# Cosine attention followed by a mixture of depths, one core: PV output of a head pair in one PSUM bank, a bank of its own for the last score block, two buffers of scaled q and k, fetched rows transposed, a new slot order

## The chip, the core and the metric

The kernel runs on one core of one Trainium2 chip. The metric is the device time of one execution in microseconds, lower is better; the number for a kernel is the median of its runs. Beside it stands one profiled execution with its trace. A span is the time from the first to the last instruction in the trace.

## What is computed

```python
def _attn_ref(q, k, v, tau):                     # 8 batches, 12 heads, 448 tokens, 64 wide
    q_n = q / (norm(q, axis=-1) + 1e-06);  k_n = k / (norm(k, axis=-1) + 1e-06)
    attn = softmax(q_n @ k_n.T / tau)            # tau = 0.1
    return attn @ v
def _moe_ref(x, w_gate, w1, w2, capacity):       # x: (8, 448, 768), F = 1024, capacity 128
    for b in range(B):
        top_idx = 128 rows of x[b] with the highest score x[b] @ w_gate
        xe = x[b, top_idx];  ye = relu(xe @ w1) @ w2
        out[b, top_idx] = xe + sigmoid(score) * ye      # other rows: out = x
```

The attention output of a batch, heads side by side, is x of the second part. All inputs and the output are fp32.

## The kernel before

**Tiling.** Two heads of a batch make a pair; there are 48 pairs, 6 per batch. The 448 tokens lie as 3 blocks of 128 and one of 64 (NC = 3, NS = 4, T = 64). Two heads share the 128 partitions of one tile: in the raw tiles head u has its tokens on partitions 64u to 64u+63, seven tokens per partition (NB7). The last 64 tokens of both heads make one shared block, so scores have four blocks: c = 0, 1, 2 hold 128 keys for each head (two matmuls, 64 rows each, side by side in the array, L275), and c = 3 holds 64 keys of both heads in one matmul (L280).

**A slot** is one pass of the loop `for i in range(N + 1)` (near the end of the function). Slot i computes the scores and exponentials of pair i, the PV product of pair i-1, the transposes of pair i+1, the scaling of pair i+2, and the squares for norms of pair i+5. The loop body writes out by hand the order in which instructions enter each engine's queue; every engine works through its own queue in that order.
- *ScalarE*: exponential of block 0 (L288), Square of a later pair's q and k (L187), in every other slot Ln and Exp for norms (L210, L211), exponential of block 3 (L291), of block 1, of block 2 (L288).
- *TensorE*: scores 0; `pv_tails` (L304: 8 matmuls, one for each query block and head, on 64 rows); sums of squares by an identity (L194); `pv` (L315: 24 matmuls of 65 columns; the 65th, a column of ones, gives the softmax sum); any mixture-of-depths work under key "A"; scores 3, 1; the 28 transposes of pair i+1 (L257); scores 2; work under key "B".
- *VectorE*: sums (L202), reciprocals (L220), `pv_evac` (L331, L333), the copy of the transposes to SBUF (L263), and the gate, rank, pick and evacuation steps of the mixture of depths (L361, L416, L424, L455, L457, L459).
- *POOL*: adds 1e-6 to norms (L217), scales q and k into the single buffer `kn` (L230), casts v (L237), casts x to bf16 (`half_x`, L354), splits gates (L371 to L374), issues the indirect DMAs (L515, L711, L726).
- *SP*: loads q, k and v (L98, L108) for a ring of 4 groups of 3 pairs, and stores x (`store_x`, L346 and L347).

**PSUM** has 8 banks: 2 score buffers of two banks (`sc`), 2 banks for the PV output (`o_ps`, one per head), one for transposes (`qkT_ps`), one for the mixture of depths (`m_ps`). The sums of squares and scores 3 live in the slot's second `sc` buffer. A second copy of the last 64 queries makes query block 3 also 128 wide: `qc(3)` is `slice(S - P, S)`, so its output lies on all partitions.

**The mixture of depths of batch b** starts when its six pairs are done, at slot s = 6(b+1), and is spread over later slots by `at(slot, key, function)`; `run(i, key)` emits what is due. The dicts `late`, `mid`, `early` and `last` give the offsets to s: four `gate` products in slots 2 to 5, `rank_rep` (scores spread to all partitions) in 5 B, `rank_count` and `pick` (a 0/1 matrix `sel`) in slot 6, `select` (row numbers and gate values of the 128 rows) in 7 A, `gather` (rows of `xh` picked and transposed in one go by matmuls with `sel`, 24 in all, L473) in 7 B and 8 A, `ffn1` twice (24 matmuls, L491), `ffn2` twice (8 matmuls of 384 columns, L500), then `scatter` (L515), which adds the rows onto `out` in DRAM. x itself has been stored to `out` by `store_x` in slot s. The last batch comes after the loop: it also stores x to `x_copy`, fetches its rows from there (L711), adds them in SBUF and writes them plainly (L726).

Of the kernel before, what the change touches and what calls it, by code (L numbers as in the profile page):

```python
# [14 lines left out]


@with_exitstack
def kernel(
# [48 lines left out]
    ps_m = ctx.enter_context(tc.tile_pool(name="ps_m", bufs=1, space=PSUM))  # L67
    sc_pool = ctx.enter_context(ExitStack())
# [13 lines left out]
    NORMS = [(0, 1), (1, 2), (3, 1), (4, 1)]  # L82
    while sum(NORMS[-1]) < N:
        NORMS.append((sum(NORMS[-1]), min(2, N - sum(NORMS[-1]))))
# [49 lines left out]
    o_ps = ps_o.tile([P, 2, 512], FP32, name="o_ps")  # L134
# [6 lines left out]
    kn = const.tile([P, 2, NB7, Dh], BF16, name="qkn")  # L141
    vo_bufs = [const.tile([P, NB7, E], BF16, name=f"vo{n}") for n in range(NB)]
    for vo in vo_bufs:
        nc.vector.memset(vo[:, :, Dh:E], 1.0)
# [8 lines left out]
    tokc = const.tile([P, NS, 2], BF16)  # L153
    for half in range(2):
        for col, base, step, mult in ((0, 0, 0, 4), (1, NC * half, 1, 3)):
            nc.gpsimd.iota(tokc[half * T:half * T + T, :, col], pattern=[[step, NS]],
                           base=base, channel_multiplier=mult,
                           allow_small_or_imprecise_dtypes=True)
# [23 lines left out]
    ss_tiles, rs_tiles, sq_tiles = {}, {}, {}  # L182

    def square(p):
        gi, g = place[p]
        sq_tiles[p] = prep.tile([P, 2, NB7 * Dh], BF16, name="sq", bufs=3)
        nc.scalar.activation(  # L187
            sq_tiles[p], raw[gi % NRAW][0][:, :, g].rearrange("p a b d -> p a (b d)"),
            AF.Square)
# [8 lines left out]
    def sum_dve(p, dst):  # L198
        n, m = nplace[p]
        if m == 0:  # L200
            ss_tiles[n] = prep.tile([P, 2, 2, NB7], FP32, name="ss")
        nc.vector.tensor_reduce(  # L202
            ss_tiles[n][:, m].rearrange("p a b -> p (a b)"),
            dst.rearrange("p (n d) -> p n d", d=D8), axis=AX.X, op=ALU.add)

    def norm_a(n):
        gn = NORMS[n][1]
        rs = prep.tile([P, 2, 2, NB7], FP32, name="rs", bufs=3)
# [10 lines left out]
    def norm_c(n):  # L219
        nc.vector.reciprocal(norm_of(n), norm_of(n))  # L220

    def scale(p, split=False):
        gi, g = place[p]
        qk = raw[gi % NRAW][0]
        n, m = nplace[p]
        rs = rs_tiles[n]
        parts = (((nc.gpsimd, 0, NC), (nc.vector, NC, NB7)) if split
                 else ((nc.gpsimd, 0, NB7),))
        for eng, b0, b1 in parts:
            eng.tensor_mul(  # L230
                kn[:, :, b0:b1], qk[:, :, g, b0:b1],
# [3 lines left out]
    def values(p):  # L235
        gi, g = place[p]
        nc.gpsimd.tensor_copy(vo_bufs[p % NB][:, :, :Dh], raw[gi % NRAW][1][:, g])  # L237
# [13 lines left out]
    def transposes(p):  # L251
        for a in range(2):
            for s in range(NB7):
                for u in range(2):
                    r = slice(u * T, u * T + T)
                    o = column(a, u, s)
                    nc.tensor.transpose(out=qkT_ps[r, o:o + T], in_=kn[r, a, s],  # L257
# [9 lines left out]
    def scores(i, c, sc=None):  # L267
        qkT = qkT_tiles[i]
        if sc is None:
# [24 lines left out]

    def qc(j):
        return slice(j * P, j * P + P) if j < NC else slice(S - P, S)

    def pv_tails(i):
        ex = exp_tiles[i]
        vo = vo_bufs[i % NB]  # L300
        for j in range(NS):
            for u in range(2):
                r = slice(u * T, u * T + T)
                nc.tensor.matmul(out=o_ps[:, u, j * E:(j + 1) * E],  # L304
                                 lhsT=ex[r, TAIL, qc(j)], rhs=vo[r, NC],
                                 start=(j == 0), stop=False, tile_position=(u * T, 0),
                                 skip_group_check=True)

    def pv(i):
        ex = exp_tiles[i]  # L310
        vo = vo_bufs[i % NB]
        for u in range(2):
            for j in range(NS):
                for c in range(NC):
                    nc.tensor.matmul(out=o_ps[:, u, j * E:(j + 1) * E],  # L315
                                     lhsT=ex[:, 2 * c + u, qc(j)],
                                     rhs=vo[:, u * NS + c], start=False,
                                     stop=(c == NC - 1), skip_group_check=True)
# [3 lines left out]
    x_last = const.tile([P, NS, P], FP32)  # L322
    xh_last = const.tile([P, NS, P], BF16)

    def pv_evac(i):
        b, hp = divmod(i, HP)
        if hp == 0:
            x_tiles[b] = xp.tile([P, NS, D], FP32, name="x_b")
        o = o_ps[:, :, :NS * E].rearrange("p u (j e) -> p j u e", e=E)
        rden = head.tile([P, NS, 2, 1], FP32, name="rden")  # L330
        nc.vector.reciprocal(rden, o[:, :, :, Dh:E])  # L331
        dst = x_last if i == N - 1 else x_tiles[b][:, :, 2 * hp * Dh:2 * (hp + 1) * Dh]
        nc.vector.tensor_mul(  # L333
            dst.rearrange("p j (u d) -> p j u d", u=2),
            o[:, :, :, :Dh], rden.to_broadcast([P, NS, 2, Dh]))

    xh_tiles, st = {}, {b: {} for b in range(B)}
# [11 lines left out]
    def half_x(i):  # L349
        b, hp = divmod(i, HP)  # L350
        if hp == 0:
            xh_tiles[b] = xp.tile([P, NS, D], BF16, name="xh", bufs=3)
# [14 lines left out]
    def rank_prep(b, eng=nc.gpsimd):  # L367
        g = gates[b % 2]
        sg = moe.tile([P, NS, 3], BF16, name="sg")
# [58 lines left out]
    def select(b):  # L428
        sel, sg = st[b]["sel"], st[b]["sg"]
        pk = bank()  # L430
        for o, w, src in ((0, 2, tokc), (2, 3, sg)):
            for j in range(NS):
                nc.tensor.matmul(out=pk[:, o:o + w], lhsT=sel[:, j], rhs=src[:, j],
                                 start=(j == 0), stop=(j == NS - 1))
        gr = moe.tile([P, 1], FP32, name="gr")
        nc.vector.tensor_reduce(gr, pk[:, 2:5], axis=AX.X, op=ALU.add)  # L436
# [3 lines left out]
        nc.vector.tensor_scalar_add(idx, pks, float(b * S))  # L440
# [323 lines left out]
```

## Time and profile before

| | us |
|---|---|
| median of 3 runs | 269.3 (267.12, 269.3, 269.72) |
| profiled execution | 268.42 |
| its span | 266.6 |
| mean granted TensorE clock in it | 0.985 of full speed |
| DMA traffic | 53.18 MB, mean 199 GB/s |
| exponentials of blocks 0 to 2 (L288), 144 of 128x896 | 917 ns each, 125.3 in sum |
| PV matmuls (L315), 1152 of 128x65 | 44.6 in sum |
| tails (L304), 384 of 64x65 | 13.9 in sum |
| scaling (L230), 48 | 1673 ns each, 80.3 in sum |
| evacuation (L333), 47 of 128x512 | 691 ns each, 32.5 in sum |
| casts of x (L354), 47 of 128x512 | 633 ns each, 29.7 in sum |

In the profile, PE stands for matmuls on TensorE, PEld for its weight loads, DVE for VectorE, ACT for ScalarE, POOL for GpSimd, SP for the queue that issues plain DMAs. A line of a timeline reads: start in us, length in us, engine, line of the program, operation, output <- inputs, shape, count, and in square brackets the idle time before it and what ended that. For a matmul "64*128" are the active rows and columns of the array and "64x448" the operand that streams through. Matmuls overlap in the pipeline, so the distance between starts is what one costs. In a list of waits the three numbers are total us, times and longest us.

### The profile page before, as it was taken

The page shows a single profiled execution, that of the slowest core. Times are in us where ns is not written, and L with a number is a line of the kernel's source. Part 1 is how long each engine was busy: PE and PEld are TensorE (multiplying, and loading weights), DVE is VectorE, ACT ScalarE, POOL GpSimd, SP SyncE. Part 2 cuts the span into 40 slices and gives each one's busy share as a digit, 9 for nine tenths or more (in the row PEclk, how much of TensorE's full clock was granted, in tenths as well). Part 3 has the DMA queues.
Part 4 walks back from the last instruction along what each step waited for, and adds up shares of the span by engine and source line. Part 5 has one row for each costly group of instructions (what it writes and reads, how often), then busy time and mean ns, then how long its engine had stood idle before and what let it go on. Part 6 is the DMA issues. An engine that isn't in the chain of part 4 may idle for free.

```text
span 266.6 us, 10588 instructions
## 1 busy us (share of the span) xinstructions
PE 225.2 (84%) x4584; PEld 169.9 (64%) x4584; DVE 175.2 (66%) x472; ACT 203.3 (76%) x322; POOL 168.3 (63%) x234
## 2 busy tenths in 40 slices
PE   7678877586899979999899979998999899989920
PEld 6456655465678557767677757866786667757810
DVE  2424445474977778858877778678876976898401
ACT  3698999897897798888888789779878986683400
POOL 5367676979766568575966667757846885743131
PEclk9999999999999999999999999999999999999995
DMA  7999999999999974799679985999580049047861
GB/s 248 285 286 279 264 254 275 368 260 259 267 285 350 235 161 64 167 276 285 130 153 262 260 203 84 216 283 274 101 192 20 2 61 210 4 61 161 255 116 63
DMA packets 32431, 53.18 MB, mean 199 GB/s; under 512 B 2176, under 2 KB 28672, under 8 KB 31488
## 3 DMA queue, kind: packets, MB, share of 16 engines
q1 hardware_dynamic: 28976, 45.13, 63.9%
q0 software_dynamic: 2992, 6.69, 14.6%
q8 instruction: 36, 0.59, 1.0%
q10 hardware_dynamic: 416, 0.69, 0.7%
q14 instruction: 11, 0.09, 0.1%
HBM read 40.11 MB, written 15.53 MB: 209 GB/s over the span
## 4 chain that ended last, share of the span: by engine, by line
PE 35%; DMA 21%; DVE 16%; ACT 12%; issue 7%; SPq 4%; POOL 3%; POOLq 1%; ACTq 0%
DMA v_raw<-in_v_dram 11%; PE m_ps L491 7%; ACT expS L288 7%; PE m_ps L500 6%; PE sc L275 6%; PE o_ps L315 5%; DVE junk L416 4%; DVE junk L361 3%; DMA qk_raw<-in_k_dram 3%; DMA qk_raw<-in_q_dram 3%; PE sc L194 3%; ACT expS L291 3%; PE qkT_ps L257 3%; DVE xeT L457 2%; DVE x_b L333 2%
## 5 line engine op out<-in xcount | busy, mean ns | idle before, releaser
L288 ACT ACTIVATE expS<-sc 128x896 bf16<-128x896 f32 x144 | 125.3, 917 | 17.0 <-PE sc L275 16.4
L230 POOL TENSOR_TENSOR qkn<-qk_raw,rs 128x896 bf16<-128x896 f32 (+1 forms) x48 | 80.3, 1673 | 36.4 <-PE qkT_ps L257 26.3
L275 PE MATMUL sc<-qkT 64*128 64x448 bf16 x288 | 52.3, 358 | 14.8 <-DVE qkT L263 7.3
L187 ACT ACTIVATE sq<-qk_raw 128x896 bf16<-128x896 f32 x48 | 45.2, 947 | 2.1 <-DMA qk_raw<-in_k_dram 2.0
L315 PE MATMUL o_ps<-vo,expS 128*128 128x65 bf16 x1152 | 44.6, 193 | 1.5 <-issue 1.5
L315 PEld LDWEIGHTS <-expS 128*128 128x128 bf16 x1152 | 40.3, 97 | 2.1 <-issue 1.7
L275 PEld LDWEIGHTS <-qkT 64*128 64x128 bf16 x288 | 15.4, 92 | 37.3 <-issue 21.0
L263 DVE COPY qkT<-qkT_ps 128x960 bf16<-128x960 bf16 x48 | 31.3, 653 | 7.8 <-PE qkT_ps L257 6.8
L291 ACT ACTIVATE expS<-sc 128x448 bf16<-128x448 f32 x48 | 25.7, 536 | 13.3 <-PE sc L280 13.2
L333 DVE TENSOR_TENSOR x_b<-o_ps,rden 128x512 f32<-128x512 f32 x47 | 32.5, 691 | 1.6
L257 PEld LDWEIGHTS <-qkn 64*64 64x64 bf16 x1344 | 24.9, 109 | 12.9 <-issue 8.4
L257 PE MATMUL qkT_ps<-iden_b,qkn 64*64 64x64 bf16 x1344 | 30.4, 194 | 3.2 <-POOL qkn L230 2.1
L354 POOL CAST xh<-x_b 128x512 bf16<-128x512 f32 x47 | 29.7, 633 | 2.0 <-DVE gr L436 1.3
L361 DVE CUSTOM_DVE_ANT_0 junk<-x_b,wg_b 128x768 bf16<-128x768 f32 (+1 forms) x32 | 30.5, 953 | 0.5 <-DMA wg_b<-in_moe_w_gate_dram 0.3
L194 PE MATMUL sc<-sq,iden_b 128*128 128x112 bf16 x384 | 26.9, 215 | 2.4 <-ACT expS L288 2.3
L202 DVE TENSOR_REDUCE ss<-sc 128x14 f32<-128x112 f32 x48 | 12.8, 273 | 24.4 <-PE sc L194 24.0
L237 POOL CAST vo<-v_raw 128x448 bf16<-128x448 f32 x48 | 26.8, 557 | 0.8 <-DMA v_raw<-in_v_dram 0.7
L217 POOL TENSOR_SCALAR rs<-rs 128x28 f32<-128x28 f32 (+1 forms) x26 | 8.0, 307 | 25.8 <-ACT rs L211 21.7
L491 PEld LDWEIGHTS <-w_sb 128*128 128x128 bf16 x384 | 22.2, 98 | 3.3 <-issue 3.1
L194 PEld LDWEIGHTS <-iden_b 128*128 128x128 bf16 x384 | 20.8, 98 | 4.6 <-issue 1.7
L416 DVE SCALAR_TENSOR_TENSOR junk<-m_ps,own,tie 128x448 bf16<-128x448 f32 (+1 forms) x28 | 19.0, 678 | 0.5
L491 PE MATMUL m_ps<-xeT,w_sb 128*128 128x128 bf16 x288 | 18.1, 219 | 1.3 <-DVE xeT L457 1.3
(90 smaller groups left out, 275.6 us busy)
## 6 DMA issues: line engine op xcount, KB each, us to landing
qk_raw<-in_q_dram SPq DMA_DIRECT2D x15, 672.0 KB, 10.1
qk_raw<-in_k_dram SPq DMA_DIRECT2D x15, 672.0 KB, 12.0
v_raw<-in_v_dram SPq DMA_DIRECT2D x30, 192.0 KB, 9.6
out_dram<-x_b SPq DMA_DIRECT2D x7, 768.0 KB, 7.8
v_raw<-in_v_dram SPq DMA_DIRECT2D x30, 144.0 KB, 9.0
out_dram<-x_b SPq DMA_DIRECT2D x7, 576.0 KB, 4.7
w_sb<-in_moe_w_dram POOLq DMA_DIRECT2D x2, 1536.0 KB, 18.9
out_dram<-x_b SPq DMA_DIRECT2D x1, 640.0 KB, 6.7
```

The costliest lines, as they stand in the source:

```text
L187: nc.scalar.activation(sq_tiles[p], raw[gi % NRAW][0][:, :, g].rearrange("p a b d -> p a (b d)"), AF.Square)
L194: nc.tensor.matmul(out=dst, lhsT=iden_b, rhs=sq[:, :, s * D8:(s + 1) * D8], start=(s == 0), stop=(s == Dh // D8 - 1))
L230: eng.tensor_mul(kn[:, :, b0:b1], qk[:, :, g, b0:b1], rs[:, m, :, b0:b1].rearrange("p a (b o) -> p a b o", o=1) .to_broadcast([P, 2, b1 - ...
L257: nc.tensor.transpose(out=qkT_ps[r, o:o + T], in_=kn[r, a, s], identity=iden_b[r, r], tile_position=(u * T, u * T))
L263: nc.vector.tensor_copy(qkT_tiles[p], qkT_ps[:, :W])
L275: nc.tensor.matmul(out=sc[:, u, :S], lhsT=qkT[r, KO + c * P:KO + (c + 1) * P], rhs=qkT[r, :S], start=True, stop=True, tile_position=(u * D ...
L288: nc.scalar.activation(ex[:, 2 * c:2 * c + 2], sc[:, :, :S], AF.Exp, scale=inv_tau)
L291: nc.scalar.activation(ex[:, TAIL], sc[:, 0, :S], AF.Exp, scale=inv_tau)
L315: nc.tensor.matmul(out=o_ps[:, u, j * E:(j + 1) * E], lhsT=ex[:, 2 * c + u, qc(j)], rhs=vo[:, u * NS + c], start=False, stop=(c == NC - 1) ...
L333: nc.vector.tensor_mul(dst.rearrange("p j (u d) -> p j u d", u=2), o[:, :, :, :Dh], rden.to_broadcast([P, NS, 2, Dh]))
L361: nc.vector.tensor_tensor_reduce(out=junk[:, d0:d1], in0=src, in1=wg_b[:, d0:d1], scale=1.0, scalar=0.0 if prev is None else prev[:, j:j + 1],
L491: nc.tensor.matmul(out=ps[:, f * CAP:(f + 1) * CAP], lhsT=w1_sb[:, t, fc * P:(fc + 1) * P], rhs=xeT[t], start=(m == 0) if cut else (t == 0 ...
```

## The change

- `o_ps` is one bank. Query blocks 0 to 2 of both heads lie side by side on 128 partitions (`o_part(u, j)`), the 64 queries of block 3 on partitions 64u to 64u+63 for head u. `qc(3)` becomes the 64 queries alone.
- The tails become three matmuls over all 128 rows for both heads at once, with a value tile padded by zeros, and two of 64 output columns. `vo` has one more block for that, and `values` makes three copies instead of one.
- `pv_evac` divides 6 blocks in one product and moves block 3 of each head by a scaled copy of 64 partitions.
- The freed bank is `ps_3`: sums of squares and scores 3 have their own buffer; scores 0, 1 and 2 take turns in the two `sc` buffers.
- `kn` becomes `kns[0]` and `kns[1]`, in turn.
- For batches 0 to 5 the picked rows are no longer gathered by matmul from `xh`: `fetch` reads them from `out` by an indirect DMA, `half_xs` casts them, `turn` transposes them with 6 transposes; `ffn2_evac` adds them in SBUF, and `scatter` writes without adding. `half_x` is left out for these batches. Batches 6 and 7 keep `gather`.
- `select` uses one tile `gtok` of row numbers and gates: 4 matmuls instead of 8.
- `ffn1` loops over t outside f, and ffn1 and ffn2 can be cut into parts (`t0`, `t1`). Names with "a" at the end are evacuated by ScalarE, ffn2 always by VectorE.
- The slot order is a list of tokens, `ORDER` (`ORDER_FIRST` for slots 0 and 1), in which MoE work has the places P1, X0, D0, D1, P1b, A0, A, X1, P2, C, D3, B; offsets of each batch stand in `PLANS`. The store of x moves to slot 3 after s, scatter to slot 15 for the first three batches, loads of w1 and w2 from slots 7 and 10 to 8 and 14.
- At the end: for batch 7, x is stored to `out` and `x_copy` in five pieces, one per slot; one of its gate products is made on POOL and ScalarE; two thirds of the last pair's PV come after the loop; the fetch from `x_copy` stands ahead of batch 6's scatter.

```diff
+ORDER = ("P1 X0 S0 D0 sums SQ E0 tails PV1 PV0 S3 D1 norms P1b A0 E3 scale S1 E1 "
+         "EV A T X1 copy P2 C S2 D3 E2 B ").split()
+ORDER_FIRST = ("P1 A S0 E0 sums D0 S2 SQ S3 tails PV0 PV1 D1 norms P1b S1 EV scale E3 "
+         "P2 E1 E2 D3 warm C T copy B ").split()
+PLANS = [{'gate': ['2D1', '3D1', '4D1', '5D1'],
+  'prep': '5P1b',
+  'rank': ['6D0', '6D1', '6D3', '6D1'],
+  'pick': '7D0',
+  'fetch': '7P2',
+  'half': '8P2',
+  'scatter': '15P2',
+  'store': '3P2',
+  'pe': [['rep', '5B'], ['select', '7A0'], ['turn', '10A'], ['f10a', '10B'], ['f11a', '13B'],
+         ['f20:0-1', '14B'], ['f20:1-8', '15X0'], ['f21:0-6', '15A'], ['f21:6-8', '15A']]},
...
-    o_ps = ps_o.tile([P, 2, 512], FP32, name="o_ps")
+    o_ps = ps_o.tile([P, 512], FP32, name="o_ps")
...
     def qc(j):
-        return slice(j * P, j * P + P) if j < NC else slice(S - P, S)
+        return slice(j * P, j * P + P) if j < NC else slice(SM, S)
+
+    def o_part(u, j):
+        if j < NC:
+            return o_ps[:, (2 * j + u) * E:(2 * j + u + 1) * E]
+        return o_ps[u * T:u * T + T, TAIL * E:(TAIL + 1) * E]
 
     def pv_tails(i):
         ex = exp_tiles[i]
-        vo = vo_bufs[i % NB]
-        for j in range(NS):
-            for u in range(2):
-                r = slice(u * T, u * T + T)
-                nc.tensor.matmul(out=o_ps[:, u, j * E:(j + 1) * E],
-                                 lhsT=ex[r, TAIL, qc(j)], rhs=vo[r, NC],
-                                 start=(j == 0), stop=False, tile_position=(u * T, 0),
-                                 skip_group_check=True)
+        vt = vo_bufs[i % NB][:, NC * E:(NC + 2) * E]
+        for j in range(NC):
+            nc.tensor.matmul(out=o_ps[:, 2 * j * E:2 * (j + 1) * E],
+                             lhsT=ex[:, TAIL, qc(j)], rhs=vt, start=(j == 0),
+                             stop=False, skip_group_check=True)
+        for u in range(2):
+            nc.tensor.matmul(out=o_part(u, NC), lhsT=ex[:, TAIL, qc(NC)],
+                             rhs=vt[:, u * E:(u + 1) * E], start=False, stop=False,
+                             tile_position=(0, u * T), skip_group_check=True)
...
+        for u in heads:
             for j in range(NS):
-                for c in range(NC):
-                    nc.tensor.matmul(out=o_ps[:, u, j * E:(j + 1) * E],
-                                     lhsT=ex[:, 2 * c + u, qc(j)],
-                                     rhs=vo[:, u * NS + c], start=False,
-                                     stop=(c == NC - 1), skip_group_check=True)
+                for c in blocks:
+                    o = (u * (NC + 2) + c) * E
+                    nc.tensor.matmul(out=o_part(u, j), lhsT=ex[:, 2 * c + u, qc(j)],
+                                     rhs=vo[:, o:o + E], start=False,
+                                     stop=(c == NC - 1),
+                                     tile_position=(0, 0 if j < NC else u * T),
+                                     skip_group_check=True)
...
         nc.vector.tensor_mul(
-            dst.rearrange("p j (u d) -> p j u d", u=2),
-            o[:, :, :, :Dh], rden.to_broadcast([P, NS, 2, Dh]))
-
+            dst[:, :NC].rearrange("p j (u d) -> p j u d", u=2),
+            o[:, :TAIL, :Dh].rearrange("p (j u) d -> p j u d", u=2),
+            rden[:, :TAIL].rearrange("p (j u) o -> p j u o", u=2)
+            .to_broadcast([P, NC, 2, Dh]))
+        for u in range(2):
+            r = slice(u * T, u * T + T)
+            nc.vector.tensor_scalar_mul(dst[T:, NC, u * Dh:(u + 1) * Dh],
+                                        o[r, TAIL, :Dh], rden[r, TAIL])
...
+    def fetch(b):
+        xs = moe.tile([P, D], FP32, name="xs")
+        st[b]["xs"] = xs
+        last = b == B - 1
+        nc.gpsimd.indirect_dma_start(
+            out=xs[:CAP], out_offset=None, in_=x_copy[:, :] if last else out_flat[:(b + 1) * S, :],
+            in_offset=bass.IndirectOffsetOnAxis(
+                ap=st[b]["row" if last else "idx"][:CAP, 0:1], axis=0))
+
+    def half_xs(b):
+        st[b]["xe"] = moe.tile([P, D], BF16, name="xe", bufs=1)
+        nc.gpsimd.tensor_copy(st[b]["xe"], st[b]["xs"])
+
+    def turn(b):
+        ps = bank().bitcast(BF16)
+        xe, xeT = st[b]["xe"], moe.tile([P, KD, CAP], BF16, name="xeT")
+        for t in range(KD):
+            nc.tensor.transpose(out=ps[:, t * CAP:(t + 1) * CAP],
+                                in_=xe[:, t * P:(t + 1) * P], identity=iden_b)
+        nc.vector.tensor_copy(xeT.rearrange("p t c -> p (t c)"), ps[:, :KD * CAP])
+        st[b]["xeT"] = [xeT[:, t] for t in range(KD)]
...
+    for hp in range(HP - 1):
+        for dst in (x_copy, None):
+            at(N - HP + 1 + hp, "P2", lambda d0=hp * P, dst=dst: store_x(
+                bb, x_tiles[bb][:, :, d0:d0 + P], d0, d0 + P, dst))
...
+    fetch(bb)
+    scatter(b)
```

## The prediction

> **What bounds the kernel now.** I read the page first, then the busy time by stage, the waits of each engine inside one steady batch, the TensorE and ScalarE order inside one pair, and last the tail. The page alone leaves two candidates:
>
> ```profile
> PE 225.2 (84%) x4584; PEld 169.9 (64%) x4584; DVE 175.2 (66%) x472; ACT 203.3 (76%) x322; POOL 168.3 (63%) x234
> ```
>
> The starts of the third-block exponential (L291) are a clock, one per pair: 12.43 us for pair 0, 92.95 for pair 17, 180.18 for pair 35, 237.14 for pair 47. Busy time cut at these four points:
>
> ```profile
> 12.43:92.95 80.52, 65.50 (x1444) 48.66 (x1443) 46.83 (x121) 70.96 (x111) 56.95 (x75) 1.00 1.08 281
> 92.95:180.18 87.23, 80.94 (x1685) 60.53 (x1683) 66.39 (x175) 72.94 (x115) 59.40 (x79) 1.00 0.82 196
> 180.18:237.14 56.96, 53.57 (x1115) 39.93 (x1114) 45.92 (x123) 45.48 (x71) 39.14 (x51) 1.00 0.47 101
> 237.14:266.60 29.46, 16.97 (x228) 13.42 (x226) 12.33 (x40) 8.27 (x18) 7.32 (x12) 0.87 0.62 146
> ```
>
> The columns are length, PE, PEld, DVE, ACT, POOL, clock, DMA share, GB/s. While only attention runs (first stage), ScalarE is busiest: 71.0 of 80.5. Once the mixture-of-depths work is woven in, TensorE is: 80.9 of 87.2, then 53.6 of 57.0. The tail is a chain. In one steady batch (122.21 to 150.63, six pairs, 28.42 us) TensorE is busy 26.84, ScalarE 24.23, VectorE 22.17, and ScalarE's waits there are for TensorE alone:
>
> ```profile
> ACT expS L291 <- PE sc L280: 2.8, 3, 1.1
> ACT expS L288 <- PE sc L275: 2.2, 3, 1.0
> ```
>
> One pair on TensorE, with an FFN block (L491) behind it:
>
> ```profile
> 138.12 0.36 PE L275 MATMUL sc<-qkT 64*128 64x448 bf16 x2
> 138.32 0.28 PE L304 MATMUL o_ps<-vo,expS 64*128 64x65 bf16 x8
> 138.54 0.57 PE L194 MATMUL sc<-sq,iden_b 128*128 128x112 bf16 x8
> 138.94 0.92 PE L315 MATMUL o_ps<-vo,expS 128*128 128x65 bf16 x24
> 139.70 0.35 PE L280 MATMUL sc<-qkT 128*128 128x448 bf16 x1
> 139.98 0.36 PE L275 MATMUL sc<-qkT 64*128 64x448 bf16 x2
> 140.28 0.63 PE L257 MATMUL qkT_ps<-iden_b,qkn 64*64 64x64 bf16 x28
> 140.84 0.36 PE L275 MATMUL sc<-qkT 64*128 64x448 bf16 x2
> 141.13 1.51 PE L491 MATMUL m_ps<-xeT,w_sb 128*128 128x128 bf16 x24
> 142.58 0.36 PE L275 MATMUL sc<-qkT 64*128 64x448 bf16 x2
> ```
>
> There is no gap in these 4.46 us. 1.45 belong to the FFN block and 0.1 to entering it, so a pair costs 2.91. The same two score matmuls take 0.20 when the next work has their tile shape (138.12, tails 64*128) and 0.29 or 0.30 when it hasn't (140.84 to 128*128; 139.98 to 64*64). Each change of shape thus costs about 0.095 us. Shapes change four times in this pair, without the FFN: tails to sums, L280 to L275, to the transposes, back.
>
> **What the Trainium skill says.** "TensorEngine Tiling (Array Packing)", Key Properties: "Changing tiling mode (not just tile) drains the TensorE". The trace agrees for every change it holds (about 0.095), including 64*128 to 64*64, where only the column side changes; it holds no 128*64 shape. "PSUM — Partial Sum Buffer", The four PSUM rules: an output stays in one bank of 512 fp32 columns; seven blocks of 65 are 455. "DMA: Bandwidth & Descriptors", SWDGE vs HWDGE vs iDMA: accumulating transfers belong to GpSimd; here the accumulating scatter holds POOL 1.6 (L515), the plain indirect ones 1.0 (L711, L726).
>
> **The change, part by part.**
>
> *PV in one bank.* The number of full PV matmuls falls from 24 to 18; six more, the third-block queries, have 64 output columns at a tile position of their own, and two of the tails too. Per pair the shapes now go: S0 64*128; sums and three tails 128*128; two tails 128*64; PV1 128*128, then 128*64; PV0 128*128, then 128*64; S3 128*128; S1; transposes; S2. That is ten changes instead of four. Streaming itself stays (24 in 0.76, 31 ns each; 8 tails in 0.22 against three of 130 columns and two of 65, about 0.2). The price of 128*128 to 128*64 isn't in the trace: from 0 (no drain for a column split) to 0.095. A gain is excluded, since streaming is no shorter. I take 0.095, because 64*128 to 64*64 pays it: 6 x 0.095 = 0.57 us per pair, 27 over 48, on the engine that bounds two stages.
>
> *Evacuation.* One reciprocal (0.19), a product of 384 in place of 512 elements (about 0.56 instead of 0.69), and two scaled copies of 64. L459 takes 614 ns for 384 with a scalar operand; L457's 412 for 256 and 672 for 512 give 1.0 ns an element, so a 64-column one is about 0.29, 0.25 back to back. VectorE: +0.3 per pair, 1.9 per batch. ffn1's evacuation moves to ScalarE (L455, 2 x 0.69 off VectorE; about 2 x 0.59 onto ScalarE, L461). The gather's evacuations (0.67 + 0.41) become one bf16 copy of 768, about 0.55 by L263 (653 ns for 960). VectorE stays near 22 per batch, ScalarE goes to 25.4.
>
> *Fetched rows.* For six batches, gather (1.07 + 0.53 us and 0.2 of shape changes) becomes six transposes, 0.33 + 0.1; select goes from 8 to 4 matmuls (0.41 to 0.2). TensorE: -1.6 per batch. POOL loses 36 casts of 0.63 (22.8), gains 48 x 0.36 in the split value copy (384 elements about 0.48, two of 64x64 about 0.22 each, against 0.56) = 17, and fetch (1.0) plus half_xs (about 0.9) six times = 11.5, less 0.6 per scatter: +2 on 168, hidden.
>
> *Queues.* The fetch waits for store b, which in SP's queue waits for scatter b-2, with later loads behind it. The loads go out at slot 6b+10 and are first squared at 6b+16, a slack of six slots; scatter landing (5.5) and stores take two to three. half_xs comes one slot after the fetch: landing 4.7 (L711 to L723) is less than a slot. Behind both in POOL stands the next scale; with two kn buffers it has about 3.4 us before the transposes need it. Cost 0, until landing passes some 8 us.
>
> *Two kn buffers, bank for S3, order.* The 26.3 us POOL waits for transposes go, but POOL bounds nothing. What counts: MoE blocks move from ahead of S3 to behind S1 or S2, so the 5.0 us per batch of ScalarE waits can shrink where TensorE has room.
>
> *Steady batch, slot by slot* (d = slot modulo 6). ScalarE alone needs 3.77, or 4.17 with norms; TensorE alone 3.48. Slack is 0.25 to 0.65, the rest of MoE adds. d0: rank counts (3 of them ahead of the copy) push qkT's copy to about 4.1 past E2, S0, sums and tails follow: 4.6. d1: select, then f11a 1.52: 5.3. d2: most of f20 (1.6): 5.0. d3: f21 1.5 between S1 and S2, with its evacuation ahead of the copy: 5.6. d4: turn and f10a 1.95: 5.5. d5: rep 0.95: 4.6. Sum 30.6, against 28.4. TensorE alone comes to 26.84 + 6 x 0.57 - 1.6 = 28.7.
>
> *Stages.* Head to 12.43: unchanged; new memsets and iotas on POOL fit before 7.16, where POOL idles 2.8 for L211. First stage: TensorE 65.5 + 17 x 0.57 - about 6 (batch 0's FFN moves on) = 69, ScalarE 71.6; waits between them fall from 9.6 to about 4.4: 76.0 (-4.5). Second: 3 x 30.6 = 91.8 (+4.6). Third: 53.6 + 12 x 0.57 + 4.6 (batch 3's f11, f20, f21 arrive here) - 3.2 (two gathers) + 0.9 of further shape changes = 62.7, with 2.0 of waits 64.7 (+7.7). Tail:
>
> ```profile
> 250.62 0.62 SPq L346 DMA_DIRECT2D x_copy<-x_last  x1
> 253.78 1.60 POOL L515 DMA_INDIRECT out_dram<-oe,idx  x1 [6.30 <-DMA x_copy<-x_last]
> 256.14 1.02 POOL L711 DMA_INDIRECT xs<-x_copy,row  x1 [0.76 <-issue]
> 260.87 1.14 DVE L723 SCALAR_TENSOR_TENSOR oe<-w_ps,gr,xs 128x384 f32<-128x384 f32 x2 [7.65 <-DMA xs<-x_copy,row]
> 262.28 1.01 POOL L726 DMA_INDIRECT out_dram<-oe,idx  x1 [5.12 <-DVE oe L723]
> ```
>
> Stores of the first five blocks now leave slot by slot, so x_copy's last part isn't queued behind them, and the fetch precedes scatter 6. It can start when row is known (L444, 250.1), not at 256.1, and xs lands about 255. Then scatter 6 (POOL to about 252.8, landing 5.6 after its start, near 257) and FFN2's end (255.1) bound the last scatter: near 257 instead of 262.3, -5.3. Span: 266.6 - 4.5 + 4.6 + 7.7 - 5.3 = 269.1. The profiled run took 268.42, 1.8 more than its span; so 270.9. The median of the runs shown (269.3) is 0.9 above that run: 271.8.
>
> **Rivals.**
> *No drain for 128*64* (22%), the other side. 27 us of TensorE time fall away. Stages: 75.0, 86.3, 58.0, tail 24.2 with the head 12.4: 255.9, or 258.6 as median. For it: no row here shows a column split at full height. Against: 64*128 to 64*64 pays. It decides below about 0.07 us per change, where the total gets under 266.6.
> *POOL stands at the fetch* (14%, slower). If xs lands 10 us after its issue (store b's landing reaches 14.4 at most), POOL holds the next scale about 2 us too long, six times: +12, 284.
> *Half a drain or better overlap* (6%): 0.05 per change takes 13 off TensorE, some 6 off the end: 265.
> *VectorE becomes the bound*: 22 of 30 per batch speaks against it beyond slot d0; folded into the first case.
>
> **Numbers.** What a measurement of this kernel can tell from no change is about 1%, 266.6 to 272.0. The main case (58%): 265 to 279; 4 faster, 24 same, 30 slower. No drain: 21 faster, 1 same. POOL: 14 slower. Half: 5 faster, 1 same. Together 0.30, 0.26, 0.44. The range 257 to 281 takes in most of no drain and part of the POOL case, leaving out under 2 in 10.
>
> **What would show it.** Gaps of about 0.1 us around the 64-column PV matmuls, so that PV takes about 1.1 us per pair instead of 0.76, prove the main step; 0.8 disproves it. L291's steady six-pair distance should be near 30.6, stage 1 near 76, the last scatter within 20 us of x_last's product. POOL waits for xs or out_dram over 3 us show the second rival. I am wrong if PV stays at 0.76, or if ScalarE still waits 5 us per batch though TensorE has room.

## The result and the profile after

The changed kernel is slower. Its median is 291.68 us (4 runs, 290.5 to 297.15), against 269.51 for the kernel before on the same chip: a ratio of 1.0822, interval 1.0718 to 1.0926. The forecast was 271.8, with a range of 257 to 281. The profiled execution took 297.15, its span is 295.4. In it TensorE's clock stood at half from 56.9 to 74.0 us, which made slots 9 to 12 take 24.6 us where four of their neighbours take 18.3; about 6 us of the span are this. It began 1.0 us after TensorE had stood idle for 1.9 us: in slot 9 the gate product stands ahead of the evacuation in VectorE's queue, and it waited for w_gate:

```profile
52.86 0.96 DVE L488 CUSTOM_DVE_ANT_0 junk<-x_b,wg_b 128x768 bf16<-128x768 f32 x1 [1.56 <-DMA wg_b<-in_moe_w_gate_dram]
```

In the other three runs, which make the ratio, the mean clock was 0.987 to 0.992 (0.960 in the profiled one), so the 6 us belong to the profile and not to the ratio. (The time of slot n is here the distance from the block-3 exponential of pair n-1 to that of pair n.)

Line numbers are now those of the changed kernel: score blocks 0 to 2 L380, block 3 L385, sums L286, tails L414 and L418, PV L429, transposes L360, their copy L366, evacuation L447 (reciprocal), L449 (product), L456 (two scaled copies), exponentials L393 and L396 (block 3), small value copies L340, fetch L609, scatter L677. The page's first lines:

```profile
PE 255.7 (87%) x4292; PEld 180.0 (61%) x4292; DVE 193.4 (65%) x561; ACT 211.0 (71%) x331; POOL 181.1 (61%) x314
```

292 matmuls fewer, and TensorE is busy 30 us longer; VectorE has 18 more. Busy time by stage, cut as before at the block-3 exponentials (L396) of pairs 0, 17, 35 and 47:

```profile
12.21:102.88 90.67, 76.67 (x1321) 52.48 (x1320) 52.60 (x148) 72.67 (x112) 56.06 (x97) 0.91 0.93 239
102.88:199.20 96.32, 90.53 (x1580) 63.42 (x1578) 71.65 (x207) 77.07 (x121) 61.12 (x104) 1.00 0.79 210
199.20:266.28 67.08, 61.39 (x1044) 42.16 (x1042) 51.06 (x141) 46.44 (x71) 46.36 (x74) 1.00 0.47 114
266.28:295.40 29.12, 18.93 (x233) 14.64 (x231) 13.32 (x44) 9.21 (x20) 10.11 (x14) 0.89 0.36 89
```

| stage | before | forecast | after |
|---|---|---|---|
| first (pairs 0 to 17) | 80.5 | 76.0 | 90.7 |
| second (17 to 35) | 87.2 | 91.8 | 96.3 |
| third (35 to 47) | 57.0 | 64.7 | 67.1 |
| tail | 29.5 | 24.2 | 29.1 |

The first stage, where the forecast had a gain, misses most. What its slots without mixture-of-depths work look like now on TensorE:

```profile
45.55 0.36 PE L380 MATMUL sc<-qkT 64*128 64x448 bf16 x2 [0.75 <-DVE qkT L366]
45.84 0.57 PE L286 MATMUL sc<-sq,iden_b 128*128 128x112 bf16 x8
46.24 0.34 PE L414 MATMUL o_ps<-vo,expS 128*128 128x130 bf16 x3
46.51 0.22 PE L418 MATMUL o_ps<-vo,expS 128*64 128x65 bf16 x2
46.66 1.28 PE L429 MATMUL o_ps<-vo,expS 128*128 128x65 bf16 x24
47.88 0.36 PE L385 MATMUL sc<-qkT 128*128 128x448 bf16 x1
48.17 0.36 PE L380 MATMUL sc<-qkT 64*128 64x448 bf16 x2
48.46 0.63 PE L360 MATMUL qkT_ps<-iden_b,qkn 64*64 64x64 bf16 x28
49.02 0.36 PE L380 MATMUL sc<-qkT 64*128 64x448 bf16 x2
50.12 0.36 PE L380 MATMUL sc<-qkT 64*128 64x448 bf16 x2 [0.73 <-DVE qkT L366]
```

PV takes 1.22 (46.66 to 47.88) instead of 0.76. Tails and PV together take 1.64 (46.24 to 47.88) instead of 0.98. At both ends TensorE stands idle for the copy of the transposes. VectorE in the same slot:

```profile
47.98 0.20 DVE L447 RECIPROCAL rden<-o_ps 128x7 f32<-128x7 f32 x1 [0.90 <-PE o_ps L429]
48.22 0.56 DVE L449 TENSOR_TENSOR x_b<-o_ps,rden 128x384 f32<-128x384 f32 x1
48.79 0.58 DVE L456 TENSOR_SCALAR x_b<-o_ps,rden 64x64 f32<-64x64 f32 x2
49.41 0.66 DVE L366 COPY qkT<-qkT_ps 128x960 bf16<-128x960 bf16 x1
```

This is a closed loop. Score block 0 to the end of PV takes 2.43 (45.55 to 47.98), the evacuation 1.43, the copy behind it in VectorE's queue 0.71, and then the next block 0 can start: 4.57 us, and these slots take 4.57 one after the other. Before, the least disturbed of them took 3.73 to 4.16. The copy could have begun when the transposes were done, near 49.1; it began 0.3 later, behind the scaled copies.

### The profile page after: what moved, and what is told of

The parts are those of the page before. It is cut to its first block, busy times and chain, and to the rows that moved or that the text cites. A ratio compares the mean times of both kernels' runs of the same rounds, so it can differ in the third digit from the quotient of the medians.

```text
span 295.4 us, 10265 instructions
## 1 busy us (share of the span) xinstructions
PE 255.7 (87%) x4292; PEld 180.0 (61%) x4292; DVE 193.4 (65%) x561; ACT 211.0 (71%) x331; POOL 181.1 (61%) x314
## 3 DMA queue, kind: packets, MB, share of 16 engines
q1 hardware_dynamic: 32816, 45.13, 57.7%
## 4 chain that ended last, share of the span: by engine, by line
PE 61%; DVE 23%; DMA 6%; issue 3%; ACT 2%; POOL 2%; POOLq 1%; SPq 0%
PE o_ps L429 15%; PE sc L380 11%; PE sc L286 7%; PE qkT_ps L360 6%; PE m_ps L639 6%; DVE qkT L366 5%; PE m_ps L651 5%; DVE junk L543 4%; PE sc L385 3%; DVE x_b L449 3%; DVE x_b L456 3%; PE o_ps L414 2%; DVE junk L488 2%; DMA out_dram<-oe,idx 2%; PE o_ps L418 2%
## 5 line engine op out<-in xcount | busy, mean ns | idle before, releaser
L393 ACT ACTIVATE expS<-sc 128x896 bf16<-128x896 f32 x144 | 128.7, 916 | 17.5 <-PE sc L380 17.4
L380 PE MATMUL sc<-qkT 64*128 64x448 bf16 x288 | 53.6, 370 | 20.1 <-DVE qkT L366 17.5
L429 PE MATMUL o_ps<-vo,expS 128*128 128x65 bf16 (+1 forms) x1152 | 63.6, 200 | 0.0
L429 PEld LDWEIGHTS <-expS 128*128 128x128 bf16 (+1 forms) x1152 | 50.3, 103 | 9.9
L396 ACT ACTIVATE expS<-sc 128x448 bf16<-128x448 f32 x48 | 26.1, 543 | 32.4 <-PE sc L385 32.3
L380 PEld LDWEIGHTS <-qkT 64*128 64x128 bf16 x288 | 13.9, 93 | 42.1 <-DVE qkT L366 26.2
L340 POOL CAST vo<-v_raw 64x64 bf16<-64x64 f32 x96 | 23.2, 242 | 21.6 <-DMA xs<-out_dram,idx 13.6
L366 DVE COPY qkT<-qkT_ps 128x960 bf16<-128x960 bf16 x48 | 31.5, 656 | 7.6 <-PE qkT_ps L360 6.7
L360 PE MATMUL qkT_ps<-iden_b,qkn 64*64 64x64 bf16 x1344 | 31.2, 197 | 2.6 <-POOL qkn L324 2.6
L360 PEld LDWEIGHTS <-qkn 64*64 64x64 bf16 x1344 | 25.8, 112 | 12.2 <-issue 5.5
L456 DVE TENSOR_SCALAR x_b<-o_ps,rden 64x64 f32<-64x64 f32 x94 | 26.7, 284 | 1.6
L286 PE MATMUL sc<-sq,iden_b 128*128 128x112 bf16 x384 | 27.6, 218 | 0.0
L449 DVE TENSOR_TENSOR x_b<-o_ps,rden 128x384 f32<-128x384 f32 x47 | 26.2, 557 | 1.6
L286 PEld LDWEIGHTS <-iden_b 128*128 128x128 bf16 x384 | 20.5, 100 | 9.0 <-issue 8.9
L333 POOL CAST vo<-v_raw 128x384 bf16<-128x384 f32 x48 | 24.4, 507 | 1.8 <-DMA v_raw<-in_v_dram 1.7
## 6 DMA issues: line engine op xcount, KB each, us to landing
qk_raw<-in_q_dram SPq DMA_DIRECT2D x15, 672.0 KB, 10.5
v_raw<-in_v_dram SPq DMA_DIRECT2D x30, 192.0 KB, 10.5
```

The source lines that it names most:

```text
L286: nc.tensor.matmul(out=dst, lhsT=iden_b, rhs=sq[:, :, s * D8:(s + 1) * D8], start=(s == 0), stop=(s == Dh // D8 - 1))
L360: nc.tensor.transpose(out=qkT_ps[r, o:o + T], in_=kns[p % 2][r, a, s], identity=iden_b[r, r], tile_position=(u * T, u * T))
L366: nc.vector.tensor_copy(qkT_tiles[p], qkT_ps[:, :W])
L380: nc.tensor.matmul(out=sc[:, u, :S], lhsT=qkT[r, KO + c * P:KO + (c + 1) * P], rhs=qkT[r, :S], start=True, stop=True, tile_position=(u * D ...
L393: nc.scalar.activation(ex[:, 2 * c:2 * c + 2], sc[:, :, :S], AF.Exp, scale=inv_tau)
L429: nc.tensor.matmul(out=o_part(u, j), lhsT=ex[:, 2 * c + u, qc(j)], rhs=vo[:, o:o + E], start=False, stop=(c == NC - 1), tile_position=(0, ...
```

## The experiments

Three causes were held against each other: the changes of tile shape on that loop (first), VectorE's longer evacuation on it (second), the new order and plans (third); the texts below call them theories 1 to 3. Later runs added a fourth, POOL standing at a landing. Ratios are to the kernel before on the same chip.

**a0, the changed kernel once more.** 

> The changed kernel once more, for a trace in which the TensorE clock is not cut. In the first trace slots without any mixture-of-depths work take 4.57 us each, and L396 starts 4.57 apart in slots 5 to 8. If that is a closed loop of engines and not the clock, the same 4.57 returns here, and the span is about 289.

One run, 296.4, its clock again at half for 13.7 us from 57.7 on, again behind a wait for w_gate (TensorE idle for 1.6 us). The slots without mixture-of-depths work took 4.57 again, at full clock, as expected; the span of 294.6 is not the expected 289. The constant slot is the kernel's; the half clock was no single accident.

**e1, all 64-column matmuls of a pair in one run**

```diff
 tails: the two 64-column matmuls left out
 pv(i): for j in range(NC)           # was range(NS)
+pv_last(i): for u in (0, 1): for c in (tail, 0, 1, 2): the eight 64-column matmuls
```

> The changed kernel with all eight 64-column matmuls of a pair in one run after the 128-column ones: two shape changes to and from 128*64 instead of six. Theory 1 (shape changes on the loop PV, evacuation, copy, scores 0, sums, tails, PV): 4 x 0.095 = 0.38 less per pair, 48 pairs, 18 us: about 273; slots without other work fall from 4.57 to about 4.2. Theory 2 (VectorE's longer evacuation ahead of the copy sets the pace): the loop still contains PV, so something is won, but less, 280 to 285. Theory 3 (new slot order and plans): at most 5 us, 286 or more.

288.43, ratio 1.0699 (1.0589 to 1.0808). TensorE in one slot:

```profile
46.13 0.34 PE L414 MATMUL o_ps<-vo,expS 128*128 128x130 bf16 x3
46.30 0.74 PE L435 MATMUL o_ps<-vo,expS 128*128 128x65 bf16 x18
46.97 0.33 PE L423 MATMUL o_ps<-vo,expS 128*64 128x65 bf16 x8
47.23 0.36 PE L385 MATMUL sc<-qkT 128*128 128x448 bf16 x1
```

The same matmuls in another order take 1.10 instead of 1.64 (46.13 to 47.23): four changes of shape less save 0.54. So it is the changes that cost, and not the 64 columns as such. Loop slots fell from 4.57 to 4.08. So the shape changes are on the path. But the total hardly moved: slot 17 took 12.1 us instead of 6.3, and the clock was at half five times before the tail. The slots did as theory 1 says; the expected 273 was missed, and the total lies where theory 3 had put it, which called for a further cause.

**e2, the kernel before with its third-block queries split to 64 columns**

```diff
-lhsT=ex[:, 2 * c + u, qc(j)]        # o_ps[:, ...]
+lhsT=ex[:, 2 * c + u, 384:448 if j == 3 else qc(j)]   # o_ps[64:, ...], tile_position=(0, 64)
```

> The kernel before, where only the third-block PV matmuls of each head are cut to 64 output columns at column position 64 (four shape changes per pair more; evacuation, order and buffers as before). Theory 1: 4 x 0.095 = 0.38 per pair of TensorE time; in the stages that TensorE bounds (about 30 pairs) that is 11 us, in the others up to 3 more: 280 to 284. Theories 2 and 3: within 2 us of before, 268 to 272.

276.78, ratio 1.031 (1.0224 to 1.0396). PV alone:

```profile
127.71 1.26 PE L316 MATMUL o_ps<-vo,expS 128*128 128x65 bf16 x24
128.90 0.36 PE L280 MATMUL sc<-qkT 128*128 128x448 bf16 x1
```

1.19 instead of 0.76, so 0.108 for each of four changes. That is 20.6 us of TensorE over 48 pairs, of which 7 reach the end, where theory 1 expected 10 or more. The first cause holds in a kernel with nothing else of the change, and costs the total less than expected.

**e3, the changed kernel with PV, tails, values and evacuation of before**

```diff
-o_ps = ps_o.tile([P, 512], FP32)    # one bank; pv_tails, pv, values, pv_evac of the change
+o_ps = ps_o.tile([P, 2, 512], FP32) # and those of before; sums and scores 3 back in sc,
+                                    # E3 earlier in the order of slots 0 and 1
```

> The changed kernel with PV, tails, value tile and evacuation of before (two output banks; sums and scores 3 share the score buffer of before), everything else changed: two scaled buffers, fetched rows, order, plans, tail. Theories 1 and 2: the loss goes, and the removed matmuls and waits show: 258 to 268. Theory 3: it stays slow, 280 or more.

274.76, ratio 1.0195 (1.0103 to 1.0287). This lies between the ranges of the theories. Some 17 of the 22 us go with the PV layout (shape changes, evacuation, value copies and the bank for scores 3 together). Some 5 stay with order, plans and fetched rows. Cut by stage, its trace takes 82.8, 88.6, 61.6 and 30.1: of the 9.0 us that it is longer than the trace of the kernel before, 4.6 lie in the third stage. The slow slots 35, 39 and 45 stay too (6.65, 8.02 and 7.45 us; 7.54, 8.06 and 8.18 in the changed kernel).

**e4, the two scaled copies behind the copy of the transposes**

```diff
 order on VectorE: reciprocal, product,
-scaled copy, scaled copy, copy of the transposes
+copy of the transposes, scaled copy, scaled copy
```

> The changed kernel, all its work kept, with the two scaled copies of 64 partitions placed behind the copy of the transposes on VectorE instead of ahead of it. If VectorE's longer evacuation stands on the closed loop (product, evacuation, copy of the transposes, score block 0), a slot without mixture-of-depths work falls from 4.57 us by the 0.3 us that the copy waited after the last transpose, to about 4.27, and the time from 291.7 to 278 to 285. If only the changes of tile shape on TensorE count, the slot stays within 0.1 us of 4.57 and the time at 289 to 293.

292.81, ratio 1.0931 (1.0798 to 1.1064): no gain. Yet the slots did as the second cause says, 4.30 instead of 4.57, and a steady batch 30.68 instead of 31.36. Slot 17 took 12.84: POOL waited 6.5 us for the fetched rows of batch 0, and TensorE stood idle from 87.4 to 93.2 but for a moment.

**e5 and e7, the FFN blocks of batches 3 to 5 spread**

```diff
-batch 3: turn 10A, f10a 10A, f11a 12B, f20 14X0, f21 14A   # likewise batches 4 and 5
+batch 3: turn 10A, f10a 10B, f11a 11B, f20 12B, f21 13A
```

> The changed kernel with the two-bank PV of before (as in e3, 274.8 us), and in batches 3 to 5 each FFN block in a slot place of its own, at key A or B, in place of the turn followed at once by FFN blocks. If the piled-up places of batches 3 to 5 are what is left of the loss, the slow slots fall from 6.65, 8.02 and 7.45 to below 6 and the time to 269 to 272. If not (TensorE has the same work to do in any order), it stays at 273 to 276.

> The changed kernel with all three repairs together: the eight 64-column matmuls of a pair in one run, the two small copies behind the copy of the transposes, and the FFN blocks of batches 3 to 5 spread. From 288.4 (one run alone) minus 48 times up to 0.3 for the copies and 3 for the plans: 270 to 280, if each cause acts by itself; slots without mixture-of-depths work 3.8 to 3.9 instead of 4.08. If the halved TensorE clock, which all runs of the one-run kernel showed, follows TensorE's density, it stays at 280 to 288 although the slots are short.

e5 took 285.97, ratio 1.068 (1.0547 to 1.0813); e7 293.9, ratio 1.1008 (1.0867 to 1.1148). (e7 has the spreading together with e1 and e4.) Both missed every range expected for the time and are worse than the kernels that they build on, e3 and e1; in e7 the loop slots did shorten, to 3.66 and 4.10. In e5 slots 39 and 45 did shorten (5.90, 6.46), but `f11` in slot 35 B needs the one bank of the mixture of depths, which the rank counts of batch 4 still read: TensorE waited 1.8 us with score block 0 behind it, and slots 36, 40, 41, 42 and 46 are longer than in e3 by 3.5, 2.4, 1.9, 1.1 and 2.4. Where these blocks stand isn't free. That the piled-up places cost anything net is not shown.

**e8, the cast of the fetched rows one slot later**

```diff
-'half': '8P2',   # batches 0, 1, 2
+'half': '9P2',
```

> The changed kernel with the cast of the fetched rows of batches 0 to 2 one slot later (9 P2 instead of 8 P2), so that POOL does not stand at the fetch. In the trace of the changed kernel the fetch of batch 0 landed 9 us after its issue and slot 17 took 1.8 us more than its neighbours; no other slot shows a POOL wait on TensorE. If that is all, 289 to 291 (2 us less); if POOL's waits of 13.6 us for fetched rows are a second cause of the loss, 284 or less; under the closed loop alone 291 to 292.

294.7, ratio 1.091 (1.0806 to 1.1015): no gain, and slot 17 took 10.5. POOL still stood at the landing (4.5 us), so the cast wasn't what waited. And the later cast now came behind POOL's next scaling and value copies: TensorE's `turn` waited 3.3 us for it. **e9** has it together with e1 and e4:

> The changed kernel with the eight 64-column matmuls of a pair in one run, the two small copies behind the copy of the transposes, and the cast of the fetched rows one slot later. In e1, e4 and e7 slot 17 took 12 to 13 us, with POOL 6.5 us at the fetch and then the TensorE clock at half. If that wait is a cause that only shows once the slots are shorter, slot 17 falls to 4.5 to 6 and the time from 288.4 to 274 to 280. If the 12 us have another source, they stay and the time is 285 to 290.

287.49, ratio 1.0622 (1.0515 to 1.073): slot 17 stayed at 12.6, as the text's second case has it. POOL's own timeline names the instruction:

```profile
80.50 1.68 POOL L624 DMA_INDIRECT xs<-out_dram,idx  x1 [0.54 <-POOL vo L340]
82.25 0.28 POOL L309 TENSOR_SCALAR rs<-rs 128x28 f32<-128x28 f32 x1
82.62 1.69 POOL L324 TENSOR_TENSOR qkn<-qk_raw,rs 128x896 bf16<-128x896 f32 x1
84.25 0.51 POOL L333 CAST vo<-v_raw 128x384 bf16<-128x384 f32 x1
84.70 0.96 POOL L340 CAST vo<-v_raw 64x64 bf16<-64x64 f32 x1
90.44 0.23 POOL L340 CAST vo<-v_raw 64x64 bf16<-64x64 f32 x1 [4.78 <-DMA xs<-out_dram,idx]
...
92.25 1.70 POOL L324 TENSOR_TENSOR qkn<-qk_raw,rs 128x896 bf16<-128x896 f32 x1
```

The second small value copy neither reads nor writes the fetched rows, and it waits for them. The trace has the wait itself: a wait for an indirect DMA's semaphore stands right ahead of this copy for 8 pairs of the changed kernel, and ahead of the first copy for one. Behind it stands the scaling of the next pair. In the changed kernel such waits come to 13.6 us for fetches and 5.6 us for scatters.

**e12 and e13, both small value copies as one product with a 0/1 mask**

```diff
-for u in range(2): tensor_copy(vo[64u:64u+64, NC + u, :64], vr[64u:64u+64, NC])
+tensor_mul(vo[:, NC:NC+2, :64], vr[:, NC] twice, mask)     # and 'half': '9P2'
```

> The changed kernel with the two small value copies of a pair replaced by one product with a 0/1 mask, and the cast of the fetched rows one slot later. In the changed kernel the second small copy carries a wait for the landing of the fetch or scatter before it, though it needs neither; the single product has no such wait. If POOL's standing there is a cause in the changed kernel, slot 17 takes 4.6 to 5.2 in place of 6.3 to 10.5 and the time is 284 to 289; if it is hidden there, 290 to 293. Slots without mixture-of-depths work stay at 4.57 in either case.

> As e9 (eight 64-column matmuls of a pair in one run, small output copies behind the copy of the transposes, cast of the fetched rows one slot later; 287.5), and the value copies as in e12, without a wait for a landing. If POOL's wait made the 12.6 us of slot 17 and the idle stretches of TensorE that half clock follows, 274 to 280, and the clock above 0.96. If e9's losses have another source, 284 to 289.

e12 (the changed kernel with these two edits) took 289.71, ratio 1.0714 (1.0645 to 1.0782): between the two ranges expected; the interval overlaps that of the changed kernel. The loop stayed at 4.57, slot 17 took 5.9. Against e8, from which it differs by the product alone, it is 5 us faster with intervals apart; so the wait did cost time once the cast stood behind it. e13 (e9 with this) took 277.93, ratio 1.0271 (1.0201 to 1.0341), clear of e9's and inside the first range expected, with the clock at 0.955 to 0.962. The same stretch of POOL in e13 (L628 is the fetch, L328 the scaling):

```profile
73.73 1.11 POOL L628 DMA_INDIRECT xs<-out_dram,idx  x1 [0.16 <-DVE gr L595]
...
76.19 1.69 POOL L328 TENSOR_TENSOR qkn<-qk_raw,rs 128x896 bf16<-128x896 f32 x1
77.82 0.51 POOL L337 CAST vo<-v_raw 128x384 bf16<-128x384 f32 x1
78.29 1.16 POOL L342 TENSOR_TENSOR vo<-v_raw,mask 128x128 bf16<-128x128 f32 x1
...
80.91 1.71 POOL L328 TENSOR_TENSOR qkn<-qk_raw,rs 128x896 bf16<-128x896 f32 x1
```

Fetch to the scaling after next takes 7.2 us instead of 11.8. The median fell by 9.6 us, but not all of that is POOL's wait. In the two traces slot 17 gives 4.7 (12.6 to 7.9); slots 9 and 10, ahead of any indirect DMA, give 6.1, because the gate product waited 4.4 us for w_gate in e9 and 1.4 in e13; slot 39 takes 3.1 back. With the slow loop the wait was nearly hidden; with the loop mended it cost some 5 us in slot 17.

**e14, e13 with w_gate loaded in slot 3 instead of 5**

```diff
-at(5, "D1", load_wg)
+at(3, "D1", load_wg)
```

> As e13, with the load of w_gate in slot 3 instead of 5. In e9 the gate product of batch 0 waited 4.4 us for it, TensorE stood idle for 4.6 us with it, and half clock for 10 us followed: slots 9 and 10 took 14.7 instead of 8. If idle and half clock come from that wait, 6 us less than e13; if the loads are only pushed back by it, no difference.

276.12, ratio 1.0196 (1.0111 to 1.0282). The wait went (slot 9: 3.66, in e13 4.49), but the interval overlaps e13's. In e13 that slot had already lost little, so this didn't test what e9's slot 9 (9.0 us) showed.

**e10, four idle stretches put into the kernel before**

```diff
+if p in (21, 27, 33, 39): 4 x tensor_mul(idle, idle, idle)   # 128x768, ahead of qkT_copy(p)
```

> The kernel before with four idle stretches of TensorE put in: in slots 20, 26, 32 and 38 VectorE multiplies a scratch tile four times (about 3 us) ahead of the copy of the transposes. No result changes. If the half-clock pieces of 3.4 us come out of TensorE's own load, they stay as they are and the time rises by 4 x 3 = 12 us at most, to 278 to 281. If idle stretches of TensorE call them up, two to four pieces of half clock stand right behind the idle stretches, and the time is 284 to 290.

298.69 (294.0 to 299.3; before 267.51 to 273.89). The products took 5.81 instead of the expected 3 us. TensorE around the first, and the page's rows of TensorE's busy tenths and granted clock in 40 slices:

```profile
112.42 1.50 PE L497 MATMUL m_ps<-xeT,w_sb 128*128 128x128 bf16 x24 [0.20 <-DVE xeT L463]
118.72 0.56 PE L281 MATMUL sc<-qkT 64*128 64x448 bf16 x2 [4.80 <-DVE qkT L269]
119.06 0.43 PE L310 MATMUL o_ps<-vo,expS 64*128 64x65 bf16 x8
119.43 0.93 PE L194 MATMUL sc<-sq,iden_b 128*128 128x112 bf16 x8
```

```profile
PE   7578786687998893998939988499857989998940
PEclk9999999699999999799977999699997999999995
```

The upper row dips in slices 16, 21, 26 and 30, and the clock in each of these or in the next. The records put half clock at 118.5 to 121.9, 152.6 to 159.4, 186.7 to 193.6 and 224.3 to 227.7, each beginning in one of the four idle stretches (4.8 us each) or at its end. The sums behind the first took 0.93 us, in the kernel before 0.57. The 284 to 290 expected for idle stretches that call up half clock were for products of 3 us; with four that are 2.8 longer they become 295 to 301, and the median lies there, 27.6 above the kernel before. In the trace slots 21, 27, 28, 33, 34 and 39 take 26.6 us more than in the kernel before, 7.4 more than the four stretches. (Slot 9 took 4.8 more in this trace for another wait for w_gate, with half clock behind it.)

**e6, e11 and e15, the parts that could help, in the kernel before**

```diff
 e6:  x of the last batch stored in five pieces, one per slot; fetch ahead of scatter 6
 e11: e6 and kns[p % 2] in place of kn
 e15: e11 and at(3, "D1", load_wg)
```

> The kernel before, with the end of the changed kernel alone: x of the last batch stored to out and x_copy in five pieces, one per slot, and the fetch from x_copy ahead of batch 6's scatter. The prediction's step for the tail says -5.3 us: 264. If the new order only swaps one wait for another, as the trace of the changed kernel suggests (2.2 us from the last product on), 267 to 268; if the ten more stores delay the loads or the last slots, no gain at all.

> The kernel before with the new end (as e6, 0.990 of before) and two buffers of scaled q and k in turn. The prediction holds that POOL's waits for the transposes bound nothing: then no difference to e6, 267 to 268. If the single buffer held the transposes back, 264 to 266.

> The kernel before with the new end and two buffers of scaled q and k (e11, 0.980 of before), and the load of w_gate in slot 3 instead of 5. In e11's trace slot 9 took 7.73 for a wait of 3.1 us on w_gate, and half clock for 3.4 us followed. If the wait goes, 3 to 4 us less: 262 to 264. If the loads behind it then come late, 266 to 268.

e6: 267.54, ratio 0.9904 (0.9855 to 0.9952). e11: 266.8, ratio 0.98 (0.9688 to 0.9913). e15: 263.79, ratio 0.9808 (0.9743 to 0.9872). All three lie 1 to 2% under the kernel before, with intervals clear of 1, e6 and e15 where their texts had a range; the steps between the three lie within their intervals. The end of e15:

```profile
238.69 0.69 DVE L333 TENSOR_TENSOR x_last<-o_ps,rden 128x512 f32<-128x512 f32 x1
248.68 1.09 POOL L712 DMA_INDIRECT xs<-x_copy,row  x1 [4.22 <-DVE gr L450]
250.07 1.59 POOL L515 DMA_INDIRECT out_dram<-oe,idx  x1 [0.30 <-issue]
256.41 1.02 POOL L728 DMA_INDIRECT out_dram<-oe,idx  x1 [4.74 <-DMA out_dram<-oe,idx]
```

From x_last's product to the last scatter 17.7 us, in the kernel before 20.6. What stands last is now scatter 6, for which the last one waited 4.7 us.

## Why the prediction was wrong

The median missed the forecast by 19.9 us. By stage the profile missed by 14.7, 4.5, 2.4 and 4.9; without the 6 us of half clock in the first stage the sum is 20.5.

- *Price of a shape change*: right. 128*128 to 128*64 and back costs as the other changes do, 0.108 (e2) and 0.135 (e1) where 0.095 was taken. Tails and PV of a pair came out 0.66 longer (1.64 for 0.98) where 0.57 was forecast. "No drain for 128*64" and "half a drain" are refuted. The Trainium skill says the same in "TensorEngine Tiling (Array Packing)", Key Properties, of any change of mode; these runs give the number.
- *Evacuation*: the terms were right (0.56 and 0.58 measured against 0.56 and 0.54), though their sum is not the "+0.3 per pair" that was carried on: 0.56 + 0.54 - 0.69 is 0.41. What failed is where they were put: "VectorE: +0.3 per pair" was held against VectorE's busy share, not against the copy behind it.
- *Slot bounds*, **the step that failed**: "ScalarE alone needs 3.77, or 4.17 with norms; TensorE alone 3.48." Each engine was summed by itself. The loop of TensorE, VectorE and TensorE again needs 4.57. Mending both of its terms (e9, e13) brings the slots back to 3.66 and 4.10, near the forecast. In the first stage a gain of 4.5 was forecast and a loss of 10.2 came, some 6 of it half clock; the 8.7 us between forecast and measurement that are left are the largest single miss. Ten slots at the loop's 4.57, where 3.77 or 4.17 was summed, make some 6 of them (an estimate).
- *Steady batch*: 30.6 forecast, 31.36 measured. From exponential to exponential 4.70, 5.30, 5.18, 5.71, 5.90, 4.57, against 4.6, 5.3, 5.0, 5.6, 5.5, 4.6 (pairs 24 to 30). There the sum by engines held. ScalarE's waits for TensorE, which the change could have shortened, stayed at 5.1 us (5.0 before), for TensorE had little room left (busy 29.85 of 31.36, where 28.7 was forecast):

```profile
ACT expS L396 <- PE sc L385: 3.6, 6, 1.4
ACT expS L393 <- PE sc L380: 1.5, 2, 1.2
```

- *Second and third stage*: 4.5 and 2.4 over. Slot 35 (7.5 us) lies in the second, slots 39 and 45 (8.1 and 8.2) in the third. e3 shows that they don't come from the PV layout. e5 shows no better place for them.
- *Queues at no cost "until landing passes some 8 us"*: the landing was taken as 4.7 us; the fetches of batches 0 to 3 landed 8.1 to 8.9 us after their issue, and POOL did stand, though at the second value copy, a wait that the split of `values` brought and no step had. POOL's own work rose by 12.8 us (168.3 to 181.1) where 2 were forecast. In the changed kernel the wait's removal moved the median by 2 us, within the intervals (e12), so "POOL stands at the fetch" is not what made it slow. It stands in slot 17, which took 12.1 to 12.8 us in e1, e4 and e9; its removal was tried on e9 alone.
- *Tail*: 5.3 forecast, 0.3 came. In the changed kernel:

```profile
272.43 0.56 DVE L449 TENSOR_TENSOR x_last<-o_ps,rden 128x384 f32<-128x384 f32 x1
...
282.83 1.05 POOL L609 DMA_INDIRECT xs<-x_copy,row  x1 [4.33 <-DVE gr L576]
284.18 1.64 POOL L677 DMA_INDIRECT out_dram<-oe,idx  x1 [0.30 <-issue]
286.97 1.14 DVE L660 SCALAR_TENSOR_TENSOR xs<-w_ps,gr,xs 128x384 f32<-128x384 f32 x2 [2.73 <-DMA xs<-x_copy,row]
290.84 1.00 POOL L677 DMA_INDIRECT out_dram<-xs,idx  x1 [5.02 <-DMA out_dram<-oe,idx]
```

  The last scatter came 18.4 after x_last's product, inside the 20 that was named as its sign, and scatter 6's landing bounds it as forecast. But the fetch went out 1.7 after the row numbers (281.13), and x_last's product came 6.2 after the exponential instead of 4.6: `f21` of batch 5 now stands in slot 47. Alone, the new end is worth 0.96% of the time (e6).
- *What is left open*: e13 is still 7 us above the kernel before. Cut by stage, its profile takes 79.1, 88.2, 68.7 and 29.7 against 80.5, 87.2, 57.0 and 29.5: the excess lies in the third stage, where slots 39 and 45 take 10.4 and 9.6 (6.3 and 5.2 before) and the clock is 0.93. What part of it the plans have and what part the half clock wasn't measured. Nor was it tried which of the parts that e3 puts back together, beside shape changes and evacuation, cost time.

## What to carry to other kernels

Sum each loop that closes over several engines, not only each engine: a term on a lightly loaded engine costs its full length when the next pass waits for what is queued behind it. Put operations of one tile shape in one run. And when a repair shortens its slots but not the time, look for the wait that the old bound had hidden.

## What the runs showed of the hardware

Half clock comes behind idle stretches of TensorE, short ones too. In the 18 profiled executions, all 45 half-clock stretches between 30 us and the tail began during a TensorE gap of at least 0.9 us or within 3.5 us of its end; they last 3.4 us or multiples. Half clock followed 16 of 53 gaps of 1.0 to 1.5 us, 10 of 21 of 1.5 to 2.5, and 15 of 17 longer ones. Of 448 gaps of 0.3 to 0.9 us it followed 12, no more than chance would give (an estimate: 45 beginnings in 4,156 us put one behind 3.8% of all moments within 3.5 us). e10 shows the direction for gaps of 4.8 us; for shorter ones only the order in time is shown. The Trainium skill describes this gate in "TensorE: Matmul & The Clock Gate", section "HAM oscillation — how this bites in real kernels", and names idle gaps over about 3.4 us as the ones to avoid; here it came behind gaps of about half that length every second time. A wait of TensorE can thus cost more than its length: 26.6 us for four stretches of 4.8 in e10.
